# Packed attention and an ELU feed-forward: ones multiplied in TensorE's early idle time, a fourth weight buffer, stores due late, and an order chosen anew

## The chip, the core and the metric

The kernel runs on one core of a Trainium2 chip. A core has five engines that run side by side, each with its own queue of instructions worked off in order: TensorE (PE, matmuls; loading a stationary operand is a row of its own, PEld), VectorE (DVE), ScalarE (ACT), GpSimd (POOL) and SyncE (SP, which here only issues DMAs). They wait for each other through semaphores. Matmul results go to PSUM, eight banks of 128 x 512 float32; everything else lives in SBUF, 128 partitions wide. DMAs are issued on SP's queue, or on ACT's or POOL's, and run on the core's 16 DMA engines.

The metric is the device time of one launch in microseconds. The kernel before takes 708.01 us, the median of three runs (707.46 to 708.13).

## The reference

```python
def sm_attn(qq, kk, vv):
    s = scale * np.matmul(qq, kk.transpose(0, 1, 3, 2))
    s = s - np.max(s, axis=-1, keepdims=True)
    a = np.exp(s)
    a = a / (np.sum(a, axis=-1, keepdims=True) + 1e-09)
    return np.matmul(a, vv)
p_packed = sm_attn(p, k, v)             # p: 8 batches, 8 heads, 32 packed queries, 64 wide
out = sm_attn(q, p_packed, p_packed)    # q, k, v: 8 batches, 8 heads, 576 tokens, 64 wide
...
h = x @ w_in                            # x: 4608 x 512, w_in: 512 x 2048
g = np.where(h > 0.0, h, np.exp(np.minimum(h, 0.0)) - 1.0)
return g @ w_out                        # w_out: 2048 x 512
```

x is the attention's output with the heads side by side, 576 rows for each of 8 batches. All is float32.

## The kernel before, in words

**Attention.** For each batch, two softmaxes. The first (s1, line 526, or in halves, line 567) lets the 32 packed queries look at 576 keys: scores, maximum (DVE), exponential (ACT, line 550), ten transposes (line 637), the product with the values (pv, line 663), a division, one more transpose (line 689). The result, `ppT`, is at once keys and values of the second softmax. Its scores (s2, line 708) are folded so that DVE can take maximum, difference, sum and product over 32 columns (lines 716 to 758), with the exponential on ACT (line 732) between. The kernel never forms x: it multiplies `ppT` with w_in (mstep, line 809) to get M, 256 rows a batch, so that h is the second softmax `a` times M.

**Feed-forward.** Hidden units come in 16 blocks f of 128. For a visit (batch, half of its tokens, first and last block), PE computes h of one block (line 1306 in plain float32, or line 1313 as three products of parts `hi` and `lo` in the fast float32 form), ACT takes relu and exp (lines 1320, 1326), DVE puts the ELU together (line 1329), ACT and DVE split it into `hi` and `lo` (`g`), and PE adds the product with w_out's block to two PSUM banks (lines 1409 to 1412), evacuated and stored at a visit's end. A later visit to the same rows adds to what lies in HBM, with an accumulating DMA on POOL's queue (line 1455). `VISITS` is the order of batches 0 and 1, which run while the weights still come in; from batch 2 on, pairs of blocks go through a scheme of Strassen's kind (lines 1044 to 1200) with seven products in place of eight, on weights combined on the chip and kept in HBM (`sw_dram`). `S_PLAINS` names pairs computed without it. Each batch leaves 64 tokens over per half; the leftovers are kept in HBM (`rest_dram`) and multiplied with the last batch.

**Weights.** w_in and w_out arrive as 64-bit numbers, one block of 512 KB a load, into a ring of three buffers `raw` (line 347). ACT or DVE take the upper bytes (lines 342 and 320, `up` and `top`), DVE puts the float32 words together (line 367); w_out's words are split into `hi` and `lo` (`wo_a` or `wo_b`, lines 320 and 381), and only then the buffer is free.

**The order of the work.** A planner in the kernel (`schedule`) fixes the order of every engine's instructions when the kernel is built. Each piece of work is an `op` with a priority (its place in the order of blocks, moved by constants such as `T_ATT`, `LOOK`, `T_SE`), planned durations on the engines that can do it, the ops it needs and the buffers it takes. Time runs in the plan; whenever an engine is free, the ready op with the lowest priority gets it. An op's end is its start, its duration, a fixed lag of its engine (`LAG`) and a lag of its own. A DMA counts as work of one engine, `DMA`. `FIRST` lists the loads that open the plan. In the plan before, PE's durations are multiplied by `COLD` (1.9) until 3 us of dense products have run. The plan is only an order: on the chip each engine waits for what its next instruction needs, however long that takes. K, v and q of a batch share a ring of two buffers (`kvq`): q's loads wait for the values' product. All loads and plain stores are issued on SP, in the plan's order.

Of the kernel before, what the change touches and what calls it, by code (L numbers as in the profile page):

```python
# [12 lines left out]
BF16 = mybir.dt.bfloat16  # L13
# [3 lines left out]
U8 = mybir.dt.uint8  # L17
# [6 lines left out]
def packed_attention_elu_ffn(  # L24
# [22 lines left out]
    nc = tc.nc  # L47
# [15 lines left out]
    ODD_HALF = (1, 0)  # L63
    HB, SW, MIX, TOP = 2, 8, 0, 2
    FC = 512
    NFC = DFF // FC
# [11 lines left out]
    VISITS = [  # L78
# [4 lines left out]
    ]  # L83
    T_ATT = [11.5, 5.0, 17.5, 8.0, 10.0, 14.0]
    T_ATT1 = [-17.0, -14.5, -14.0, -6.0, -18.5, -13.0]
    LI = 4.0
    LO = 2.0
    LM = 1.0
    LOOK = 4.25
    TM = [26.5, 32.5, 37.5, 36.5]  # L90
    FIRST = "q v i3 k i0 i1 i2 o2".split()
    COLD = 1.9
    T_S2 = -8.0
    STAY = 19
    SWITCH = 0.105
    F_PLAIN = 0
    H_PLAIN = [0, 1]
    T_WS = 11
    T_AS = 6
    S_PLAIN = []  # L100
    S_PLAINS = {
        (2, 0): [7], (2, 1): [0], (3, 0): [1], (3, 1): [0], (4, 0): [0, 4], (4, 1): [1],
        (5, 0): [0], (5, 1): [0], (6, 0): [4], (6, 1): [7],
    }
    T_SW7 = 36
    T_ATTS = {3: [-2.5, -1.5, -5.5, 8.5, 12.0, 21.0], 4: [-1.5, 7.5, 13.5, 3.5, 10.0, 23.0], 5: [-6.5, 4, -10.5, -3.5, 12.5, 28.0], 6: [5, 10, 14.0, 3.5, 11.5, 24.5], 7: [1.0, -10, -5, 3.5, 11.5, 23.0]}
    TMS = {3: [19, 30.0, 34.5, 30.0], 4: [22, 19.5, 26.0, 27.0], 5: [11.5, 28.5, 29.0, 29.0], 6: [23, 18.5, 28.0, 23.0], 7: [16.5, 35, 30.0, 31.5]}
    T_RL = 21.0
    T_RX = 2.0
    T_HS = 20.5  # L110
    S_FIRST = (2, 0)
    T_SW = 7.5
    T_SL = 6.5
    T_SE = 15.0
    LOOK_S = 5.5
# [54 lines left out]

    def op(prio, on, fn, deps=(), take=(), use=(), after=(), mode=None, lag=0):
        o = Op()
        o.lag = lag
        o.prio, o.on, o.fn, o.deps = prio, on, fn, [d for d in deps if d is not None]
        o.after = [d for d in after if d is not None]
        o.take, o.end, o.n, o.mode = list(take), None, len(ops), mode
        for b in list(take) + list(use):
            b.users.append(o)
        ops.append(o)
        return o  # L180

    def schedule():
# [25 lines left out]
        while todo:  # L208
            for n, o in enumerate(todo[:400]):
# [12 lines left out]
                if e == "PE":  # L222
                    if dense < 3.0:
                        cost *= COLD
                        o.on = {e: cost}
                        dense += cost * (o.mode is None and cost > 1.0)
                    cost += SWITCH * (o.mode != mode)
                    mode = o.mode
                idle_at[e] = now + cost + GAP[e]
                o.start, o.end = now, now + cost + LAG[e] + o.lag  # L230
                for x, needs in o.next:
                    x.wait -= 1
                    if needs:
                        x.ready = max(x.ready, o.end)
                for r in {id(b.ring): b.ring for b in o.take}.values():
# [5 lines left out]
            else:  # L241
                ends = [o.end for o, _ in out[-400:] if o.end > now]
                ends += [t for t in idle_at.values() if t > now]
# [45 lines left out]
    for x in top_ts:  # L289
# [40 lines left out]
    def weights(f, first, prio):  # L330


        raw = ring_tile("raw", stg, [P, 8 * WC + 8], U8, "raw", bufs=3)
        up_b = ring_tile("up", stg, [P, WC], U16, "up")
# [51 lines left out]
        t = FIRST.index(name) - 60 if name in FIRST else prio - 8  # L386
        ld = op(t, {"DMA": 1.45}, load, take=[raw])
        x = op(prio, {"ACT": 0.63, "DVE": 0.42}, lift, [ld], take=[up_b], use=[raw])
# [28 lines left out]
    def attention(b, ts):  # L417
# [54 lines left out]
        def load_k(e, n):  # L472
            if n == 0:
                nc.sync.dma_start(out=p_b.t, in_=pT[b])
            if b == 0:
                nc.sync.dma_start(out=k_b[0].t, in_=kT[b])
            else:
                nc.sync.dma_start(
                    out=k_b[n].t[:, :2 * S].rearrange("p (c s) -> p c s", c=2),
                    in_=kT[b, :, 2 * n:2 * n + 2, :],  # L480
                )

        def load_v(e, n):
            x = v_b[n].t
            nc.sync.dma_start(
                out=x[:, :2 * E].rearrange("p (c e) -> p c e", c=2),
                in_=v[b, 2 * n * P:2 * (n + 1) * P, :].rearrange("(c p) e -> p c e", p=P),
            )
            nc.sync.dma_start(
                out=x[:S - 4 * P, 2 * E:], in_=v[b, 4 * P:, n * E // 2:(n + 1) * E // 2]  # L490
            )

# [431 lines left out]
    def strassen_weights(u):  # L924
# [35 lines left out]
        for n, b in enumerate(sw):  # L960
# [13 lines left out]
            y = op(prio, {"DVE": 0.41}, low, [y], use=[t_b, b])  # L974
            s_ready[u, n] = op(prio, {"DMA": 0.7}, store, [y], use=[b])

# [14 lines left out]
    def keep_leftover(b, f, o, prio):  # L991
        run["hb"] = o
        hb_done[b].append(o)
        if f % 2:
            x = hb[b]

            def store(e):
                nc.sync.dma_start(out=rest_dram[b // 4, f // 2, :, :, b % 4 // 2, b % 2, :], in_=x.t)

            rest_done[b, f // 2] = op(prio - T_HS, {"DMA": 0.5}, store, hb_done[b], use=[x])  # L1000

# [11 lines left out]
    def strassen_pair(i, b, win, f):  # L1013
# [210 lines left out]
        if last:  # L1224
# [37 lines left out]
            y = op(q, {"DVE": 0.42}, add3, [y], use=[part, acc[1]])  # L1262
            y = op(q, {"DVE": 0.69}, add4, [y, acc[2].last], use=[part, acc[2]])
            y = op(q, {"DVE": 0.42 if both or rest else 0.69}, add5, [y, acc[3].last], use=[part, acc[3]])
# [5 lines left out]

            def store(e):
                for r in range(2):
                    nc.sync.dma_start(
                        out=out[t0 + r * step:t0 + r * step + P, :], in_=part.t[:, r * E:(r + 1) * E]
                    )

            op(q, {"DMA": 1.4}, store, [y], use=[part])

    acc = None
    for i, (b, win, f) in enumerate(order):  # L1280
# [140 lines left out]
        if final:  # L1421
# [25 lines left out]
            for a, (r0, r1) in zip(acc, rows):  # L1447
# [59 lines left out]
```

## Time and profile before

| | |
|---|---|
| median of three runs | 708.01 us (707.46 to 708.13) |
| the profiled execution's own time | 708.88 us |
| its span, first to last instruction | 706.3 us |
| mean granted clock of TensorE | 0.987 |
| DMA | 167.79 MB, 238 GB/s over the span |

The span is 2.6 us shorter than the execution that it belongs to; what lies around it is start and end of the launch. A busy PE in the profile is not always a PE at its peak: the ends of matmuls are modelled, and a matmul of the same shape takes about twice as long while the granted clock is 0.5.

Three groups of the page show the size of the instructions that fill most of the span: `L1200 PE MATMUL psum<-sw,g` with 1212 instructions and 183.7 us, `L1135 DVE TENSOR_TENSOR g<-w,g` with 96 and 99.6 us, `L320 ACT CAST g<-w` with 96 and 86.6 us. The DMA part of the page has 340 loads of combined weights of 256 KB each (3.9 us from issue to landing), 32 loads of weights of 512 KB (4.6 and 4.8 us), and 22 accumulating stores on POOL's queue (5.4 us).

### The profile page before, as it was taken

Reading aid. Unit: us, or ns where it says so; the run is one execution under the profiler, and the core shown is the slowest. Engines: PE = TensorE matmul, PEld = TensorE weight load, DVE = VectorE, ACT = ScalarE, POOL = GpSimd, SP = SyncE. Lnnn points to the kernel's source line nnn. Section 1 sums busy time; section 2 is a strip of 40 time slices with the busy share of each in tenths; the row PEclk is TensorE's granted clock in tenths of the full one; section 3 lists DMA queues with packets and bytes.
Section 4 is the critical chain, followed back from the end, with each engine's and each line's share of the span. In section 5 each row is a group of like instructions: output and inputs, shape, how many; then the busy total and the mean of one; then the engine's idle time right before and its main releaser. Section 6 shows DMA issues by size and latency. Waiting matters only on the chain.

```text
span 706.3 us, 16075 instructions
## 1 busy us (share of the span) xinstructions
PE 675.5 (96%) x6051; PEld 593.9 (84%) x6051; DVE 576.3 (82%) x1284; ACT 454.8 (64%) x888; POOL 21.1 (3%) x30
## 2 busy tenths in 40 slices
PE   3599998998999999999999999999999999999996
PEld 2376886785879988998989988898899988999996
DVE  1898665998988998778987879779986999878874
ACT  4899998785667557755674557665665566555441
POOL 0000011102010000000000000000000000000000
PEclk9889999999999999999999999999999999999999
DMA  8877777579399956969788777798788787675863
GB/s 324 279 238 248 237 196 153 122 203 290 125 268 295 314 182 199 318 194 312 245 262 267 242 212 231 240 274 270 250 285 299 224 274 235 194 219 158 293 206 124
DMA packets 102797, 167.79 MB, mean 238 GB/s; under 512 B 26176, under 2 KB 35392, under 8 KB 102464
## 3 DMA queue, kind: packets, MB, share of 16 engines
q1 hardware_dynamic: 99552, 160.99, 70.5%
q0 software_dynamic: 3168, 5.77, 5.3%
q8 instruction: 48, 0.79, 0.4%
q14 instruction: 29, 0.24, 0.1%
HBM read 138.94 MB, written 27.79 MB: 236 GB/s over the span
## 4 chain that ended last, share of the span: by engine, by line
PE 83%; ACT 6%; DMA 5%; DVE 3%; issue 1%; SPq 1%; DVEq 0%; ACTq 0%
PE psum L1200 40%; PE psum L1044 22%; PE psum L809 4%; PE psum L1313 4%; PE psum L1409 3%; PE psum L1410 2%; PE psum L1412 2%; DMA raw<-in_w_out 2%; PE psum L663 2%; DMA raw<-in_w_in 1%; PE psum L1306 1%; DMA kvq<-in_qT 1%; PE psum L708 1%; PE psum L637 1%; PE psum L567 1%
## 5 line engine op out<-in xcount | busy, mean ns | idle before, releaser
L1200 PE MATMUL psum<-sw,g 128*128 128x256 f32 x1212 | 183.7, 283 | 0.0
L1200 PEld LDWEIGHTS psum<-sw,g 128*128 128x128 f32 x1212 | 160.7, 189 | 9.5 <-issue 7.0
L1135 DVE TENSOR_TENSOR g<-w,g 128x896 fp32r<-128x896 f32 (+1 forms) x96 | 99.6, 1039 | 28.4 <-ACT g L320 28.0
L320 ACT CAST g<-w 128x896 fp32r<-128x896 f32 (+1 forms) x96 | 86.6, 903 | 52.9 <-PE psum L1200 23.4
L1044 PE MATMUL psum<-a_hi,m_hi 128*128 128x256 f32 (+1 forms) x384 | 115.5, 301 | 0.0
L1044 PE MATMUL psum<-a_hi,m_lo 128*128 128x256 f32 (+1 forms) x384 | 113.5, 296 | 0.0
L1044 PE MATMUL psum<-a_lo,m_hi 128*128 128x256 f32 (+1 forms) x384 | 113.4, 295 | 0.0
L1200 PE MATMUL psum<-wo_a,g 128*128 128x256 f32 (+1 forms) x537 | 90.7, 299 | 0.4 <-ACT e L1059 0.4
L1126 DVE TENSOR_TENSOR w<-w 128x128 f32<-128x128 f32 (+1 forms) x255 | 84.8, 333 | 6.4
L1200 PE MATMUL psum<-wo_b,g 128*128 128x256 f32 (+1 forms) x534 | 84.8, 288 | 0.0
L1200 PEld LDWEIGHTS psum<-wo_a,g 128*128 128x128 f32 x537 | 75.9, 189 | 5.8 <-issue 1.8
L1044 PEld LDWEIGHTS psum<-a_hi,m_hi 128*128 128x128 f32 x384 | 72.7, 189 | 8.7 <-issue 2.7
L1056 ACT ACTIVATE e<-psum 128x320 f32<-128x320 f32 x96 | 41.7, 436 | 57.4 <-PE psum L1044 54.9
L1200 PEld LDWEIGHTS psum<-wo_b,g 128*128 128x128 f32 x534 | 73.1, 189 | 4.5 <-issue 3.4
L1044 PEld LDWEIGHTS psum<-a_lo,m_hi 128*128 128x128 f32 x384 | 72.6, 189 | 0.2
L1044 PEld LDWEIGHTS psum<-a_hi,m_lo 128*128 128x128 f32 x384 | 72.6, 189 | 0.0
L1056 ACT ACTIVATE w<-psum 128x512 f32<-128x512 f32 x48 | 28.6, 598 | 41.4 <-PE psum L1044 23.4
L1051 DVE SCALAR_TENSOR_TENSOR w<-e,psum 128x256 f32<-128x256 f32 x96 | 39.8, 415 | 15.8 <-ACT e L1059 15.5
L1059 ACT ACTIVATE e<-e 128x320 f32<-128x320 f32 x96 | 45.1, 472 | 2.6
L822 DVE TENSOR_TENSOR m_lo<-psum,m_hi 128x1024 fp32r<-128x1024 f32 (+1 forms) x36 | 37.1, 1038 | 7.1 <-ACT m_hi L320 7.1
L1051 DVE SCALAR_TENSOR_TENSOR w<-w,psum 128x512 f32<-128x512 f32 x48 | 32.5, 678 | 10.5 <-ACT w L1059 10.3
L320 ACT CAST m_hi<-psum 128x1024 fp32r<-128x1024 f32 (+1 forms) x36 | 31.1, 875 | 12.0 <-PE psum L809 11.3
(121 smaller groups left out, 1156.7 us busy)
## 6 DMA issues: line engine op xcount, KB each, us to landing
sw<-sw_dram SPq DMA_DIRECT2D x340, 256.0 KB, 3.9
raw<-in_w_in SPq DMA_DIRECT2D x16, 512.0 KB, 4.6
kvq<-in_v SPq DMA_DIRECT2D x16, 512.0 KB, 5.7
raw<-in_w_out SPq DMA_DIRECT2D x16, 512.0 KB, 4.8
out<-part SPq DMA_DIRECT2D x32, 256.0 KB, 3.4
sw_dram<-sw SPq DMA_DIRECT2D x32, 256.0 KB, 5.5
kvq<-in_kT SPq DMA_DIRECT2D x14, 576.0 KB, 5.0
kvq<-in_qT SPq DMA_DIRECT2D x14, 576.0 KB, 5.5
```

Of the source, the lines that this page charges most:

```text
L320: (nc.scalar.copy if e == "ACT" else nc.vector.tensor_copy)(out=out, in_=in_)
L809: nc.tensor.matmul(ps.t[cols_of(pair), g, :w], lhsT=st.ppT.t[rows_of(g), pair, :], rhs=w_in_sb[rows_of(g), pair, c * FC + part * w:c * FC ...
L822: nc.vector.tensor_tensor(out=m_b[1].t[:, :, fs], in0=ps.t[:, :, :w], in1=m_b[0].t[:, :, fs].bitcast(F32), op=ALU.subtract,)
L1044: nc.tensor.matmul(ps, lhsT=m_b[p].t[:, g, o:o + P], rhs=st.a.t[q][:, g, cols], start=(n == 0), stop=(n == 3 * G - 1),)
L1051: nc.vector.scalar_tensor_tensor(out=out, in0=e_, scalar=-1.0, in1=ps, op0=ALU.add, op1=ALU.max)
L1056: nc.scalar.activation(out=out, in_=ps, func=AF.Relu, scale=-1.0)
L1059: nc.scalar.activation(out=x, in_=x, func=AF.Exp, scale=-1.0)
L1126: nc.vector.tensor_tensor(out=out, in0=x, in1=y, op=o)
L1135: nc.vector.tensor_tensor(out=g_b.all[:, 7 * P:(7 + b1 - b0) * P], in0=blocks(b0, b1), in1=g_b.all[:, :(b1 - b0) * P].bitcast(F32), op=ALU ...
L1200: nc.tensor.matmul(a.t[:, at * H:at * H + rhs.shape[-1]], lhsT=operand(blk, p), rhs=rhs, start=new and n == k == 0, stop=a.final == (u, mi ...
L1313: nc.tensor.matmul(ps_b.t[:, :n_tok], lhsT=m_b[x].t[:, g, o:o + P], rhs=st.a.t[y][:, g, cols], start=(n == 0), stop=(n == 3 * G - 1),)
L1409: nc.tensor.matmul(a.t, lhsT=g_b.t[0][:, t], rhs=wo(f, 0), start=first, stop=False)
```

## The change

Ten edits.

1. **Ones.** The tile `part_sb` is filled with ones by DVE at the start. Read as bfloat16, its first 256 columns are both operands of a matmul into a PSUM bank that nothing reads (`fill`). From 1.5 us of planned time on, whenever nothing else is planned for PE, the planner puts in one such matmul, of a planned 0.11 us, until dense products (h or w_out's, over 0.6 us each) of 3 us in all have been planned. Then the bank is given back. `COLD` is gone: real work is planned at its full-clock durations.
2. **Late stores.** Ops can be `late`: whoever needs such an op, or the buffers that it uses, counts on its end; dependents add 1.5 us. Stores get it, except the last batch's.
3. **Accumulating stores** count as 1.7 us of DMA with 2.8 us of lag, in place of 1.0 us of POOL. They are still issued on POOL's queue.
4. **Four buffers** for arriving weights, in place of three, with 0.4 us of lag for a load.
5. **v in one transfer.** The host lays v out so that each half is one load with 5 KB in each partition (64 KB of it padding), in place of two loads.
6. **p of batch 0** is issued on ACT's queue.
7. **The store of a Strassen visit** is two ops of one DMA each: rows 128 to 255 after the fourth addition, rows 0 to 127 after the fifth. Before, both were issued after the fifth.
8. **Leftovers' stores** count as 0.3 us in place of 0.5.
9. **One more pair plain** at visit (2, 0), and another pair plain at (6, 0).
10. **Order and due times** chosen anew: three neighbouring pairs of visits swap, and nearly all constants of the priorities differ.

```diff
-        (0, 0, 0, 4), (0, 1, 0, 4), (1, 0, 0, 4), (1, 1, 0, 4),
+        (0, 0, 0, 4), (0, 1, 0, 4), (1, 1, 0, 4), (1, 0, 0, 4),
         (1, 1, 4, 8), (1, 0, 4, 8), (0, 1, 4, 8), (0, 1, 8, 12),
-        (0, 0, 4, 8), (0, 0, 8, 12), (1, 0, 8, 12), (0, 1, 12, 16),
-        (1, 1, 8, 16), (1, 0, 12, 16), (0, 0, 12, 16),
+        (0, 0, 4, 8), (0, 0, 8, 12), (0, 1, 12, 16), (1, 0, 8, 12),
+        (1, 1, 8, 16), (0, 0, 12, 16), (1, 0, 12, 16),
...
-    FIRST = "q v i3 k i0 i1 i2 o2".split()
-    COLD = 1.9
+    FIRST = "i2 k q v i1 i3 i0".split()
+    T_FILL = 1.5
...
-    T_RL = 21.0
-    T_RX = 2.0
-    T_HS = 20.5
+    T_RL = -3.0
+    T_RX = 0.5
+    T_HS = 41.5
...
+    def fill(e):
+        x = part_sb[:, 0, :E // 4].bitcast(BF16)
+        nc.tensor.matmul(fill_b.t[:, :E // 2], lhsT=x[:, :P], rhs=x, start=True, stop=True)
...
                     if dense < 3.0:
-                        cost *= COLD
-                        o.on = {e: cost}
-                        dense += cost * (o.mode is None and cost > 1.0)
+                        dense += cost * (o.mode is None and cost > 0.6)
+                        fill_end.end = now if dense >= 3.0 else None
...
-                        x.ready = max(x.ready, o.end)
+                        x.ready = max(x.ready, o.end + x.late)
...
+                if fill_end.end is None and now >= T_FILL and idle_at["PE"] <= now:
+                    o = Op()
+                    o.on, o.fn, o.deps, o.mode, o.lag = {"PE": 0.11}, fill, [], None, 0
...
+                    out.append((o, "PE"))
+                    continue
...
+    nc.vector.memset(part_sb[:, 0, :], 1.0)
...
-        raw=3, up=2, top=TOP, p=2, ppT=2, pp=1, k0=1, q0=1,
+        raw=4, up=2, top=TOP, p=2, ppT=2, pp=1, k0=1, q0=1,
...
-                nc.sync.dma_start(out=p_b.t, in_=pT[b])
+                (nc.sync if b else nc.scalar).dma_start(out=p_b.t, in_=pT[b])
...
-            x = v_b[n].t
...
+            nc.sync.dma_start(out=v_b[n].t, in_=v[b, n])
...
+            for r, z in ((1, y4), (0, y)):
+                op(q, {"DMA": 0.7}, lambda e, r=r: store(e, r), [z], use=[part], late=LATE * (b < B - 1))
...
-                eng = {"POOL": 1.0} if visits[v_n][2] > 0 else {"DMA": 0.7}
-                stores[r0] = op(i + LOOK, eng, store, [y, stores.get(r0)], use=[part])
+                again = visits[v_n][2] > 0
+                stores[r0] = op(
+                    i + LOOK, {"DMA": 1.7 if again else 0.7}, store, [y, stores.get(r0)], use=[part],
+                    lag=2.8 * again, late=LATE,
+                )
```

More of the change, by code (lines that the diff above doesn't have):

```diff
@@ L64, in packed_attention_elu_ffn @@
     HB, SW, MIX, TOP = 2, 8, 0, 2
+    LATE = 1.5
     FC = 512
@@ L78, in packed_attention_elu_ffn @@
     VISITS = [
[1 row of a table removed]
[1 row of a table added]
         (1, 1, 4, 8), (1, 0, 4, 8), (0, 1, 4, 8), (0, 1, 8, 12),
[2 rows of a table removed]
-    ]
[L84 to L90, printed above, removed]
-    FIRST = "q v i3 k i0 i1 i2 o2".split()
-    COLD = 1.9
-    T_S2 = -8.0
-    STAY = 19
[2 rows of a table added]
+    ]
+    T_ATT = [5.5, 0.5, 17.0, 10.0, -5.5, 16.0]
+    T_ATT1 = [-22.0, -10.5, -21.5, -13.5, -21.5, -9.0]
+    LI = 3.5
+    LO = 1.5
+    LM = 1.5
+    LOOK = 4.0
+    TM = [25.5, 32.5, 37.0, 33.5]
+    FIRST = "i2 k q v i1 i3 i0".split()
+    T_FILL = 1.5
+    T_S2 = -21.0
+    STAY = 15
     SWITCH = 0.105
@@ L169, in packed_attention_elu_ffn, with op @@
     LAG = {"PE": 0.27, "DVE": 0.05, "ACT": 0.05, "DMA": 2.2, "POOL": 5.0, "CTL": 0.0}
-    def op(prio, on, fn, deps=(), take=(), use=(), after=(), mode=None, lag=0):
+    def op(prio, on, fn, deps=(), take=(), use=(), after=(), mode=None, lag=0, late=0):
         o = Op()
-        o.lag = lag
+        o.lag, o.late = lag, late
         o.prio, o.on, o.fn, o.deps = prio, on, fn, [d for d in deps if d is not None]
@@ L241, in schedule @@
             else:
-                ends = [o.end for o, _ in out[-400:] if o.end > now]
+                if fill_end.end is None and now >= T_FILL and idle_at["PE"] <= now:
+                    o = Op()
+                    o.on, o.fn, o.deps, o.mode, o.lag = {"PE": 0.11}, fill, [], None, 0
+                    o.late, o.prio, o.n = 0, 0, 0
+                    o.take = [] if fill_b.users[1:] else [fill_b]
+                    if o.take:
+                        if not R["psum"].grant(o.take, now):
+                            raise ValueError
+                        R["psum"].take(o.take, now)
+                    fill_b.users.append(o)
+                    o.start, o.end = now, now + 0.11
+                    idle_at["PE"] = o.end
+                    out.append((o, "PE"))
+                    continue
+                ends = [o.end + t for o, _ in out[-700:] for t in (0, LATE) if o.end + t > now]
                 ends += [t for t in idle_at.values() if t > now]
@@ L330, in weights @@
     def weights(f, first, prio):
-        raw = ring_tile("raw", stg, [P, 8 * WC + 8], U8, "raw", bufs=3)
+        raw = ring_tile("raw", stg, [P, 8 * WC + 8], U8, "raw", bufs=4)
         up_b = ring_tile("up", stg, [P, WC], U16, "up")
@@ L386, in weights @@
         t = FIRST.index(name) - 60 if name in FIRST else prio - 8
-        ld = op(t, {"DMA": 1.45}, load, take=[raw])
+        ld = op(t, {"DMA": 1.45}, load, take=[raw], lag=0.4)
         x = op(prio, {"ACT": 0.63, "DVE": 0.42}, lift, [ld], take=[up_b], use=[raw])
@@ L974, in strassen_weights @@
             y = op(prio, {"DVE": 0.41}, low, [y], use=[t_b, b])
-            s_ready[u, n] = op(prio, {"DMA": 0.7}, store, [y], use=[b])
+            s_ready[u, n] = op(prio, {"DMA": 0.7}, store, [y], use=[b], late=LATE)
     for u in range(NF // 2):
@@ L998, in store @@
                 nc.sync.dma_start(out=rest_dram[b // 4, f // 2, :, :, b % 4 // 2, b % 2, :], in_=x.t)
-            rest_done[b, f // 2] = op(prio - T_HS, {"DMA": 0.5}, store, hb_done[b], use=[x])
+            rest_done[b, f // 2] = op(
+                prio - T_HS, {"DMA": 0.3}, store, hb_done[b], use=[x], late=LATE
+            )
     def g_buf():
@@ L1262, in strassen_pair @@
             y = op(q, {"DVE": 0.42}, add3, [y], use=[part, acc[1]])
-            y = op(q, {"DVE": 0.69}, add4, [y, acc[2].last], use=[part, acc[2]])
+            y = y4 = op(q, {"DVE": 0.69}, add4, [y, acc[2].last], use=[part, acc[2]])
             y = op(q, {"DVE": 0.42 if both or rest else 0.69}, add5, [y, acc[3].last], use=[part, acc[3]])
@@ L1269, in strassen_pair, with store @@
                 run["rest5"].deps.append(acc[3].last)
[L1271 to L1277, printed above, removed]
+            def store(e, r):
+                nc.sync.dma_start(
+                    out=out[t0 + r * step:t0 + r * step + P, :], in_=part.t[:, r * E:(r + 1) * E]
+                )
+            for r, z in ((1, y4), (0, y)):
+                op(q, {"DMA": 0.7}, lambda e, r=r: store(e, r), [z], use=[part], late=LATE * (b < B - 1))
     acc = None
@@ L1484, in pairs_T, with values @@
         )
+    def values(x):
+        out = np.zeros((B, 2, 128, 2 * E + E // 2), x.dtype)
+        for n in range(2):
+            for c in range(2):
+                out[:, n, :, c * E:(c + 1) * E] = x[:, (2 * n + c) * 128:(2 * n + c + 1) * 128]
+            out[:, n, :S - 512, 2 * E:] = x[:, 512:, n * E // 2:(n + 1) * E // 2]
+        return out
     arrays = {
@@ L1488 @@
         "in_kT": pairs_T(k),
-        "in_v": np.ascontiguousarray(v.transpose(0, 2, 1, 3).reshape(B, S, H * D)),
+        "in_v": values(v.transpose(0, 2, 1, 3).reshape(B, S, H * D)),
         "in_pT": pairs_T(p),
```

31 lines of the change are left out of this document (14 added, 17 removed).

## The prediction

> **What bounds the kernel now.** I read the page first, then the stretches by stage, the granted clock at single places, the chain of waits, and the timeline of the head and the tail. The page:
>
> ```profile
> span 706.3 us, 16075 instructions
> PE 675.5 (96%) x6051; PEld 593.9 (84%) x6051; DVE 576.3 (82%) x1284; ACT 454.8 (64%) x888; POOL 21.1 (3%) x30
> ```
>
> TensorE (PE) is the bound: 96% of the span. A change like this can only win where PE stands idle or runs slowly, so I cut the span into stretches; the columns are length, then busy time of each engine, granted clock, DMA share.
>
> ```profile
> core 0: us, PE busy (x) PEld busy (x) DVE busy (x) ACT busy (x) POOL busy (x), PEclk, DMA share, GB/s
> 0.00:35.00 35.00, 16.91 (x265) 10.19 (x269) 18.44 (x38) 22.14 (x46) 1.62 (x8) 0.93 0.85 300
> 35.00:40.00 5.00, 5.00 (x72) 4.00 (x64) 4.28 (x11) 4.46 (x12) 0.00 (x0) 0.50 0.71 243
> 40.00:110.00 70.00, 68.12 (x454) 52.25 (x454) 55.25 (x127) 67.12 (x155) 3.67 (x4) 1.00 0.73 221
> 110.00:120.00 10.00, 7.44 (x39) 6.21 (x38) 4.68 (x13) 7.01 (x17) 0.82 (x2) 0.93 0.66 191
> 120.00:170.00 50.00, 50.00 (x461) 40.67 (x468) 48.13 (x121) 38.46 (x98) 8.04 (x10) 0.98 0.76 183
> 170.00:180.00 10.00, 7.73 (x77) 4.36 (x62) 7.05 (x16) 5.49 (x11) 1.76 (x2) 0.83 1.03 318
> 180.00:700.00 520.00, 519.63 (x4706) 475.78 (x4705) 436.19 (x961) 310.09 (x554) 5.23 (x6) 1.00 0.76 241
> 700.00:706.30 6.30, 0.68 (x6) 0.47 (x5) 2.24 (x5) 0.00 (x0) 0.00 (x0) 0.95 0.43 166
> ```
>
> The 520 us from 180 on have 0.4 us of idle PE: nothing to win. What is lost lies in four places: the head (18.1 us idle of 35, then 5 us at half clock), 110 to 120 (2.6 idle), 170 to 180 (2.3 idle), the tail (5.6 idle). From 40 to 110 ACT is nearly as full as PE (67.1 and 68.1 of 70), so there a faster PE alone wins little. The granted clock around these gaps:
>
> ```profile
> 19.00:23.00 4.00, 3.53 (x64) 1.78 (x64) 3.09 (x6) 2.65 (x6) 0.00 (x0) 0.58 0.98 350
> ...
> 40.00:42.00 2.00, 2.00 (x16) 1.33 (x23) 1.85 (x4) 2.00 (x6) 0.00 (x0) 0.97 1.11 401
> ...
> 119.00:122.00 3.00, 3.00 (x10) 2.71 (x11) 1.94 (x5) 3.00 (x8) 1.75 (x2) 0.50 0.58 53
> 122.00:123.00 1.00, 1.00 (x6) 0.75 (x4) 0.61 (x2) 0.86 (x3) 0.00 (x0) 0.98 1.05 191
> ```
>
> The chain of waits (start, us) says when PE took up work before those stretches, and how long two matmul groups take at full clock:
>
> ```profile
> 34.50 2.31 PE psum L663 x72
> ...
> 118.94 1.65 PE psum L1313 x6
> ...
> 147.93 1.13 PE psum L526 x32
> ...
> 163.65 1.39 PE psum L663 x80
> ```
>
> After an idle gap the clock is 0.5 and comes back only after continuous work: PE restarts at 118.9 and is at 0.98 in 122 to 123, some 3.4 us later; it restarts at 34.5, is at 0.50 all through 35 to 40 and at 0.97 in 40 to 42, some 5.6 us later. Timeline of PE in the head:
>
> ```profile
> 7.92 2.17 PE L526 MATMUL psum<-k,p 64*32 64x288 f32 x32 [7.92 <-DMA k<-in_kT]
> 12.20 2.37 PE L637 MATMUL psum<-ident,tmp 128*128 128x128 f32 x10 [2.10 <-ACT tmp L550]
> 14.49 2.42 PE L663 MATMUL psum<-kvq,tmp 128*32 128x64 f32 x80
> ...
> 27.15 1.97 PE L1306 MATMUL psum<-k,m_hi 128*128 128x256 f32 x8 [0.47 <-DVE k L758]
> 30.72 1.49 PE L637 MATMUL psum<-ident,tmp 128*128 128x128 f32 x10 [1.61 <-ACT tmp L550]
> ```
>
> So the head runs cold: 2.17 against 1.13 for the first scores, 2.42 against 1.39 for the values, and for ten transposes 2.37 against 1.49 at 30.7. (The clock column has 0.93 over the first 35 us; the durations say that it does not see all of this.)
>
> **The change, part by part.**
>
> **1. Ones in the head.** What they can save on the chain from k's landing to the first dense product at 27.15: scores 1.04, transposes 0.88 (half of it on the chain, since the first group of five is evacuated while the second runs: 0.45), values 1.03, and half a microsecond of the second scores at 19 to 21 us (clock 0.58 there). Together about 3.0. After that, 35 to 40 at clock 0.50 loses 2.5 us of full-clock work, and 34.5 to 35 another 0.25: 2.75 in all. ACT is 4.46 of 5 busy and DVE 4.28 there, so not all of it passes: I take 2.0.
>
> What they cost. A one is planned at 0.11 us. No row has it; nearest is the dense stream:
>
> ```profile
> 683.35 15.57 PE psum L1200 x132
> ```
>
> 0.118 us for 256 columns at full clock, about 0.236 at half. The ones are a fixed number, issued in order ahead of real work, so PE must get through all of them. They are planned from 1.5 us of the planner's time, which I set 0.7 behind the span's (estimate), so from 2.2; up to k's landing at 7.92 fit 52. At full clock they take 6.1 us; the cold stretch adds half of 3.4 to 5.6 us, 1.7 to 2.8. They need only one 128x512 memset on an idle DVE and start somewhere between 1 and 2.2 (I take 1.6), so they end at 9.4 to 10.5: the first scores start 1.5 to 2.6 late, I take 2.1. Some 90 more lie between there and the fourth dense product (estimate: about 16 us idle in all by then, over 0.11, less 52); at 0.008 over plan each, 0.7. So 3.0 + 2.0 - 2.8: a **gain of 2.2**. Bounds: a loss of 1 (nothing passes ACT and DVE, wake-up at its slowest) and a gain of 5 (the whole 2.75, wake-up in 3.4 us, ones at plan).
>
> The Trainium skill ("TensorE: Matmul & The Clock Gate", Part 1: The HAM clock gate) says that the clock needs one full busy window of about 3.4 us, and that the windows run freely. By it the wake-up would take 3.4 to 6.8 us and the ones would end up to 0.6 us later than by my rows; the sum would fall by 0.3. The 3.4 and 5.6 us above agree.
>
> **2. Four weight buffers.**
>
> ```profile
> 108.40 6.49 DMA raw<-in_w_out
> ```
>
> ```profile
> 114.91 0.65 ACT L342 ACTIVATE up<-raw 128x512 uint16<-128x512 uint8 x1 [2.99 <-DMA raw<-in_w_out]
> ```
>
> ```profile
> L347 SPq DMA_DIRECT2D raw<-in_w_out x11: 328/337/592, 49.4 to 112.1; - x11
> L347 SPq DMA_DIRECT2D raw<-in_w_in x10: 323/336/541, 41.9 to 99.7; - x10
> ```
>
> The load at 108.4 waited for its buffer, took 6.5 us, and ACT stood 2.99 us; PE then idled 2.5 and ran 3.4 us at half clock. Price 2.6 + 1.7 = 4.3. The 21 loads from 41.9 to 112.1 come one per 3.5 us, so a fourth buffer gives 3.5 us of lead, more than 2.99. What is late next is ACT's own work (67.1 of 70 us busy before it), so I take **3.0** (0 to 4.3). In the head the fourth buffer lets the last of the first four loads be issued without waiting for a conversion; the DMA is at its rate there (share 0.85 over 35 us, 300 GB/s), and q's transfer covers it, so I count nothing; without that cover it would be one load, 1.7 us (512 KB at 300 GB/s).
>
> **3. Stores due late, accumulating stores counted as transfers, new order.** These add no instruction, but move loads.
>
> ```profile
> 165.76 7.47 DMA kvq<-in_qT
> ```
>
> q of a batch waits until the values' matmuls free its buffer, then takes 7.5 us among stores; in 170 to 180 PE idles 2.27, and the clock of 0.83 loses 1.7: 4.0. The new accounting tells the planner of that traffic, but the ring of two buffers remains and stays the cause. I take **1.5** (-2 to 4). Three neighbouring pairs of visits swap, and batch 1's loads, queued on SP among weight loads and stores, move with their due times. The leftovers' call is due 24 places later than before (behind its use, no longer ahead); it can still go early, since the DMA has room (share 0.76 from 180 on, 0.43 at the end); uncovered it would stop PE by at most a load like the 6.5 us one above, less its lead.
>
> One more pair is computed plain: 12 matmuls in place of 21.
>
> ```profile
> 391.01 2.79 PE psum L1200 x12
> ```
>
> 21 at 0.118 are 2.48 us: **+0.3**, on PE's path.
>
> **4. v in one transfer, p on ACT's queue, two halves of a store.** v's two issues become one: 16 fewer on SP, off the path; each carries 64 KB of padding, 16 x 64 KB = 1 MB, 3.5 us of transfer at 300 GB/s over the run, hidden where the DMA share is 0.76. p's issue goes to an ACT that idles 12.9 of the first 35 us; nothing. The tail:
>
> ```profile
> 701.26 1.01 DVE L1231 TENSOR_TENSOR part<-part,psum 128x512 f32<-128x512 f32 x2
> 701.37 0.81 SPq L1273 DMA_DIRECT2D out<-kvq  x2
> 702.30 0.89 SPq L1273 DMA_DIRECT2D out<-part  x2
> ```
>
> Both last issues wait for the last addition; afterwards only one does: **0.45** saved (0 to 0.45).
>
> **Sum.** -2.2 - 3.0 - 1.5 + 0.3 - 0.45 = -6.9. The profiled execution took 708.9 (span 706.3); 702.0 there. The median of 708.0 lies 0.9 below the profiled run, so **701.1**; own range 696 to 706, from the bounds taken not all at once.
>
> **Rivals.**
>
> *ACT and DVE hold the head.* PE's new speed is swallowed by them: 67.1 of 70 us on ACT from 40 to 110 speaks for it, 12.9 us of idle ACT before 35 against. The head gives 0, q's stall stays: 708.0 - 3.0 - 0.45 + 0.3 = **704.9**.
>
> *The change doesn't do what it says.* The ones stop at 3 us of dense products, PE idles again and is cold; the new order has its own late load where the old ones were, since SP issues in order and a load behind a waiting store gains nothing from a fourth buffer. Only the tail and the plain pair stay: **707.9**. For it: the clock was 0.50 in 35 to 40 although dense products had run at 27.15. Against it: 2.99 us of ACT's wait has a plain cause.
>
> *Slower: the ones are a queue in front of real work.* If PE stays at half clock under them, each takes about 0.236. The other parts bring 4.65, so it is slower than before from a lateness of 4.65 plus the noise, 6 us, at the fourth product: over 140 ones that is 0.11 + 0.045, a mean above 0.155. At 0.17 it is 8.4 late with nothing won: 708.0 - 4.65 + 8.4 = **711.8**. For it: PE was cold at 14.5 after 4.5 us of work with a gap in it. Against: at 118.9 it woke in 3.4 us of plain matmuls.
>
> **How the numbers follow.** Forecast 0.62, ACT and DVE 0.17, doesn't do it 0.09, slower 0.10, a larger gain than the own range (both stalls and the whole head) 0.02. A measurement of this kernel can tell about 0.2%, 1.4 us: faster is below 706.6. Faster takes the forecast, the larger gain, most of the second (0.14) and a little of the third (0.03): 0.81; same 0.09; slower 0.10. The range leaves out half the slow case and the far end of gains: 695 to 710.
>
> **What would show it.** Right: first scores last near 1.13, clock 1.00 through 20 to 42, the first dense product ahead of 27 us, no ACT wait of 3 us on a weight near 110, one issue behind the last addition. Wrong: first scores later than 10.6 (ones too slow); clock 0.5 in 30 to 40; PE idle as long as before in 100 to 180; PE idle beyond 180, where the order had none.

## The result and the profile after

The changed kernel takes **700.18 us** (median of four, 699.53 to 701.61) against 708.07 us for the kernel before (median of four, 707.46 to 709.32): a ratio of 0.9889, 95% interval 0.9869 to 0.9909, 7.9 us less. The profiled execution took 700.24 us. Its page begins:

```profile
span 698.2 us, 16294 instructions
PE 686.1 (98%) x6197; PEld 604.8 (87%) x6197; DVE 573.6 (82%) x1282; ACT 455.3 (65%) x888; POOL 21.1 (3%) x30
```

PE is busier than before although the kernel is shorter: the ones count as work. So the stretches matter, not the sum. The view by windows of the kernel after (length, then busy time of each engine, granted clock, DMA share):

```profile
core 0: us, PE busy (x) PEld busy (x) DVE busy (x) ACT busy (x) POOL busy (x), PEclk, DMA share, GB/s
0.00:35.00 35.00, 32.77 (x482) 24.99 (x483) 20.21 (x44) 23.52 (x49) 1.62 (x8) 1.00 0.86 325
35.00:40.00 5.00, 3.21 (x19) 2.41 (x17) 4.12 (x9) 5.00 (x13) 0.00 (x0) 1.00 0.84 273
40.00:110.00 70.00, 68.53 (x479) 51.90 (x480) 55.17 (x127) 68.02 (x155) 3.67 (x4) 1.00 0.78 232
110.00:120.00 10.00, 9.48 (x53) 8.00 (x52) 7.47 (x18) 9.82 (x24) 1.75 (x2) 1.00 0.52 96
120.00:170.00 50.00, 49.95 (x461) 40.26 (x461) 49.51 (x129) 35.49 (x92) 8.67 (x10) 1.00 0.84 224
170.00:180.00 10.00, 10.00 (x59) 8.74 (x58) 9.93 (x25) 6.48 (x18) 0.00 (x0) 1.00 0.68 186
180.00:690.00 510.00, 509.66 (x4633) 466.20 (x4632) 423.42 (x930) 306.57 (x543) 5.36 (x6) 1.00 0.76 243
```

Two of the four losing places are gone. In 110 to 120 PE idles 0.5 us in place of 2.6, and the 3.4 us at half clock behind that gap (1.7 us of work) are gone too: 3.7 us. In 170 to 180 it idles not at all in place of 2.3 us, at clock 1.00 in place of 0.83: 4.0 us. The span shrank by 8.1, so with the 0.3 us of the plain pair about 0.7 us is left for everything else, the head included.

The head, PE's timeline of the kernel after:

```profile
1.46 5.22 PE L185 MATMUL psum<-part 128*128 128x256 bf16 x27 [1.46 <-DVE ebias L297]
7.45 1.20 PE L539 MATMUL psum<-k,p 64*32 64x288 f32 x32 [0.77 <-DMA k<-in_kT]
8.59 2.47 PE L185 MATMUL psum<-part 128*128 128x256 bf16 x21
...
13.71 1.46 PE L676 MATMUL psum<-kvq,tmp 128*32 128x64 f32 x80
...
25.16 1.03 PE L1321 MATMUL psum<-k,m_hi 128*128 128x256 f32 x4
...
37.18 1.02 PE L1321 MATMUL psum<-k,m_hi 128*128 128x256 f32 x4
40.39 0.72 PE L721 MATMUL psum<-kvq,ppT 64*32 64x288 f32 x16 [2.19 <-DMA kvq<-in_qT]
```

and the same two last pieces of work in PE's timeline of the kernel before:

```profile
40.81 1.03 PE L1306 MATMUL psum<-k,m_hi 128*128 128x256 f32 x4
41.76 0.72 PE L708 MATMUL psum<-kvq,ppT 64*32 64x288 f32 x16
```

The scores last 1.20 us in place of 2.17, the values 1.46 in place of 2.42, and the first dense product starts at 25.16 in place of 27.15. The lead grows to 3.6 us (40.81 less 37.18). Then PE stands 2.19 us for q of batch 1, a wait that before did not have, and the lead is 1.4 us. The chain of waits of the kernel after runs through that transfer:

```profile
33.48 6.78 DMA kvq<-in_qT
```

The stall at 170 to 180 went another way. SP's queue in the kernel before, then in the kernel after:

```profile
165.07 2.07 SPq L497 DMA_DIRECT2D kvq<-in_qT  x2
```

```profile
156.88 1.39 SPq L510 DMA_DIRECT2D kvq<-in_qT  x2
```

PE's timeline before, where the second half of the scores waits for that q, and after, from the values' product that frees the buffer to the scores:

```profile
173.37 1.21 PE L708 MATMUL psum<-kvq,ppT 64*32 64x288 f32 x16 [2.27 <-DMA kvq<-in_qT]
```

```profile
155.40 1.46 PE L676 MATMUL psum<-kvq,tmp 128*32 128x64 f32 x80
...
164.37 1.20 PE L721 MATMUL psum<-kvq,ppT 64*32 64x288 f32 x32
```

The new order has the values' product at 155.4, 8.2 us earlier than before (163.65 in the prediction's chain). So q is issued 8.2 us earlier, other products fill the 7.5 us from its issue to the scores, and all 32 score matmuls follow without an idle gap on PE.

The tail: the chain of waits ends, before and after, in the same addition on DVE:

```profile
701.94 0.33 DVE part L1231
```

```profile
693.80 0.33 DVE part L1246
```

```profile
694.29 0.41 SPq L1287 DMA_DIRECT2D out<-part  x1
```

Only one issue stands behind it now, as the third fence shows (SP's queue after, a view cut to 694.3 to 694.9; the other of the pair was issued at 693.86). Yet from that addition to the end of the span it is 4.4 us in both kernels (706.3 less 701.94, 698.2 less 693.80).

### The profile page after: what moved, and what is told of

It is laid out like the page before. It is cut to its first block, busy times and chain, and to the rows that moved or that the text cites. A ratio compares the mean times of both kernels' runs of the same rounds, so it can differ in the third digit from the quotient of the medians.

```text
span 698.2 us, 16294 instructions
## 1 busy us (share of the span) xinstructions
PE 686.1 (98%) x6197; PEld 604.8 (87%) x6197; DVE 573.6 (82%) x1282; ACT 455.3 (65%) x888; POOL 21.1 (3%) x30
## 4 chain that ended last, share of the span: by engine, by line
PE 91%; ACT 4%; DVE 2%; DMA 2%; issue 1%; DVEq 0%; SPq 0%; ACTq 0%
PE psum L1215 41%; PE psum L1059 22%; PE psum L822 5%; PE psum L1328 4%; PE psum L1424 3%; PE psum L1425 3%; PE psum L1427 3%; PE psum L185 2%; PE psum L676 2%; PE psum L1321 2%; PE psum L721 1%; PE psum L650 1%; DMA kvq<-in_qT 1%; PE psum L580 1%; DMA k<-in_kT 1%
## 5 line engine op out<-in xcount | busy, mean ns | idle before, releaser
L1215 PE MATMUL psum<-sw,g 128*128 128x256 f32 x1200 | 179.0, 282 | 0.0
L1215 PEld LDWEIGHTS psum<-sw,g 128*128 128x128 f32 x1200 | 157.6, 189 | 7.3 <-issue 4.7
L1215 PE MATMUL psum<-wo_a,g 128*128 128x256 f32 (+1 forms) x543 | 93.8, 304 | 0.0
L1215 PEld LDWEIGHTS psum<-wo_a,g 128*128 128x128 f32 x543 | 77.9, 189 | 7.0 <-issue 2.6
L1215 PEld LDWEIGHTS psum<-wo_b,g 128*128 128x128 f32 x519 | 71.5, 189 | 4.9 <-issue 3.9
L822 PE MATMUL psum<-w_in_sb,ppT 64*32 64x512 f32 (+1 forms) x640 | 35.8, 513 | 0.0
```

The lines of the kernel that those rows point to most:

```text
L822: nc.tensor.matmul(ps.t[cols_of(pair), g, :w], lhsT=st.ppT.t[rows_of(g), pair, :], rhs=w_in_sb[rows_of(g), pair, c * FC + part * w:c * FC ...
L1215: nc.tensor.matmul(a.t[:, at * H:at * H + rhs.shape[-1]], lhsT=operand(blk, p), rhs=rhs, start=new and n == k == 0, stop=a.final == (u, mi ...
```

## The experiments

Each kernel was timed beside the kernel before on the same chip; ratios are to that, with 95% intervals. 0.001 is 0.7 us. "In the order of" a kernel means that each engine's instructions are exactly that kernel's but for the edit.

**Without the ones, in the order of after.**

```diff
-        nc.tensor.matmul(fill_b.t[:, :E // 2], lhsT=x[:, :P], rhs=x, start=True, stop=True)
+        return
```

> The kernel after, with the same order of every other instruction, but the 167 ones are not issued. Theory A (the prediction's step 1: ones save about 5 us of cold time and cost about 2.8, net 2.2): the time rises by about 2, to 702.4, the first scores take 2.2 us again and the clock shows 0.5 in places before 40 us. Theory B (the order behind the head was chosen for a warm head, so the whole cold time of 5 to 6 us comes back): 705 to 706. Theory C (the head is held by transfers, ACT and DVE, and the ones buy nothing): 699.5 to 700.9, no change that can be told.

702.11 us, ratio 0.9933 (0.991 to 0.9957), 0.0044 or 3.1 us slower than with them (0.9 to 5.3 by the two intervals). Its windows and PE's waits show part of it:

```profile
160.00:170.00 10.00, 8.63 (x97) 5.54 (x96) 9.50 (x21) 5.51 (x13) 1.76 (x2) 1.00 0.95 285
```

```profile
PE psum L822 <- DVE w_in_sb L387: 3.6, 1, 3.6
PE psum L721 <- DMA kvq<-in_qT: 2.9, 3, 1.6
```

The wait for q at 165 us comes back: 1.4 us of the 10 are idle, where after has 0.05 in 50. In the head, the scores of batch 1 start at 40.52, hardly later than the 40.39 of after: there the late q had eaten the difference already. So the ones are worth some 3 us in this order, and in these profiles half of it is seen some 130 us behind them. Why there stays open: from 41 to 160 us PE is only 0.1 us later at the same matmul than in after, and q was issued 0.1 us later, but its two halves took 8.0 and 8.9 us to land, in after 5.3 and 7.1.

**Each one twice, in the order of after.**

```diff
         nc.tensor.matmul(fill_b.t[:, :E // 2], lhsT=x[:, :P], rhs=x, start=True, stop=True)
+        nc.tensor.matmul(fill_b.t[:, :E // 2], lhsT=x[:, :P], rhs=x, start=True, stop=True)
```

> The kernel after with every one issued twice, the order otherwise the same: some 170 ones of 0.11 us more, 18.7 us of added work for TensorE in the head. If the ones are a queue in front of real work (the slower rival of the prediction), nearly all of the added time after the first scores shows: the 27 added ones ahead of the scores find 0.8 us of slack plus a warmer clock, the other 140 have none, so plus 13 to 16 us, 713 to 716. If ACT, DVE and transfers hold the head and TensorE has slack between its pieces, less than 8 us shows: below 708.

717.31 us, ratio 1.0153 (1.0126 to 1.0181): 0.0264 or 18.7 us above after, more than the 13 to 16 expected. The 167 added ones would be 18.7 us at the 0.112 us that one takes at full clock (33 in 3.71 us in the chain of after). So about all of what they take ends up in the time: ones do queue in front of real work, and a plan that gives them too short a duration pays for it. At 0.112 against a planned 0.11 it doesn't.

**Every second one left out, in the order of after.**

```diff
+    nth = itertools.count()
+
     def fill(e):
+        if next(nth) % 2:
+            return
```

> The kernel after with every second one left out, all else in place. If the ones cost time where they stand in front of real work (prediction: 0.7 us for being longer than planned), this is up to 1 us faster than after, as long as the clock stays at 1.00. If the clock falls because TensorE is then idle half of the time between its pieces, it goes the way of the kernel without ones, 2 to 3 us slower than after (ratio to before 0.992 to 0.993).

699.52 us, ratio 0.9897 (0.9874 to 0.9921): the same as after. PE's timeline:

```profile
1.46 3.17 PE L189 MATMUL psum<-part 128*128 128x256 bf16 x14 [1.46 <-DVE ebias L301]
7.43 2.17 PE L543 MATMUL psum<-k,p 64*32 64x288 f32 x32 [2.80 <-DMA k<-in_kT]
```

The first scores run cold here (2.17, in after 1.20), and only from 10.3 us on are ones as short as at full clock. Even so, batch 1's second scores start at 37.96, in after at 40.39: fewer ones stand in front of them. At 163.8 PE waits 1.0 us for the same q as without the ones, which takes half of its lead over after. So the time needs neither warm first scores nor every gap filled.

**Ones in the plan of before.** The planner of before, with the ones added to it as in the change, and all else left (`COLD` too).

```diff
+                if fill_end.end is None and now >= 1.5 and idle_at["PE"] <= now:
+                    o = Op()
+                    o.on, o.fn, o.deps, o.mode, o.lag = {"PE": 0.11}, fill, [], None, 0
...
+                    out.append((o, "PE"))
+                    continue
...
+    nc.vector.memset(part_sb[:, 0, :], 1.0)
```

> The kernel before with ones in the idle time of its own order (its planned durations stay the cold ones, so every other instruction keeps its place), until 3 us of dense products are planned. Theory A: about 2 us faster than before, 706, clock 1.00 up to the last one. Theory B (the ones carry most of the gain): 4 to 6 us faster, 702 to 704. Theory C (the head is held by others): within 1 us of before, 707 to 709.

709.82 us, ratio 1.006 (1.0029 to 1.0091). The expectation's premise did not hold: the planner, which now gives a bank to the ones and has more points in planned time, made another order (some 800 of PE's 6051 real matmuls are not those that stand at the same place in before), so this run says nothing of the ones alone. PE's timeline of its profile shows one thing all the same:

```profile
1.46 5.75 PE L184 MATMUL psum<-part 128*128 128x256 bf16 x30 [1.46 <-DVE ebias L299]
10.00 2.18 PE L548 MATMUL psum<-k,p 64*32 64x288 f32 x32 [2.79 <-DMA k<-in_kT]
```

With 2.8 us of idle time behind 30 ones the scores ran as slowly as with no ones (2.17).

**Ones alone, in the order of before.** 122 ones put into the idle gaps of before's plan, into banks that stand free there.

```diff
-        for o, e in schedule():
+        for o, e in with_ones(schedule()):
```

> The kernel before in exactly its order on every engine; only 122 ones are put between TensorE's instructions, where its plan has idle time from 4.05 us on up to the fourth dense product. This is edit 1 alone. Prediction's step 1: 2 us faster than before (ratio 0.997), bounds 5 faster to 1 slower. If the ones only pay in an order chosen for a warm head: within 1 us, or slower by 1 to 3 as the ones stand in front of work that comes sooner than its cold plan says.

707.39 us, ratio 1.0007 (0.9993 to 1.0021): nothing. PE's timeline, then ACT's, then PE's waits:

```profile
7.60 1.21 PE L527 MATMUL psum<-k,p 64*32 64x288 f32 x32 [0.85 <-DMA k<-in_kT]
...
13.55 1.46 PE L664 MATMUL psum<-kvq,tmp 128*32 128x64 f32 x80
...
20.55 2.17 PE L709 MATMUL psum<-q,ppT 64*32 64x288 f32 x32
```


```profile
14.90 0.67 ACT L343 ACTIVATE up<-raw 128x512 uint16<-128x512 uint8 x1 [1.81 <-DMA raw<-in_w_in]
...
17.58 0.65 ACT L343 ACTIVATE up<-raw 128x512 uint16<-128x512 uint8 x1 [1.17 <-DMA raw<-in_w_in]
18.14 0.29 ACT L676 ACTIVATE pp<-psum,ri 128x64 f32<-128x64 f32 x1
```

```profile
PE psum L690 <- ACT pp L676: 3.0, 1, 3.0
```

The scores last 1.21 us and the values start at 13.55 in place of 14.49. But in before's order two conversions of weights stand on ACT ahead of the division. They wait for weights, so the division ends no earlier than with a cold PE (18.14, before 17.30), and the second scores start at 20.55, before at 19.18. Six ones (1.15 us) stand in front of them too, and after the 3.0 us of idle time they run at half clock (0.50 from 19.9 to 23.0). The head's gain is lost at an engine that works in order behind a transfer.

**Four buffers alone, in the order of before.**

```diff
-        raw = ring_tile("raw", stg, [P, 8 * WC + 8], U8, "raw", bufs=3)
+        raw = ring_tile("raw", stg, [P, 8 * WC + 8], U8, "raw", bufs=4)
```

> The kernel before in exactly its order, but four real buffers for arriving weights, so each load on SP's queue waits for one release earlier. This is edit 4 alone. Prediction's step 2: 3 us faster (ratio 0.996), ACT's wait of 3 us near 112 to 115 and TensorE's idle time at 116 to 119 are gone. Rival: the load stands behind other waiting instructions on SP's queue in the old order, so it is issued no earlier and the time stays within 1 us; the wait then went away through the new order.

703.04 us, ratio 0.9945 (0.9922 to 0.9968): 3.9 us faster. Its windows:

```profile
110.00:120.00 10.00, 9.54 (x53) 7.98 (x52) 5.79 (x16) 8.71 (x22) 1.75 (x2) 1.00 0.79 183
120.00:170.00 50.00, 47.15 (x468) 36.81 (x474) 49.22 (x124) 37.47 (x94) 8.88 (x10) 1.00 0.79 199
170.00:180.00 10.00, 10.00 (x72) 7.65 (x57) 7.08 (x15) 5.01 (x11) 0.00 (x0) 0.83 0.89 285
```

The stall at 110 to 120 is gone: at the same matmuls PE's lead over before grows there from 1.3 us (at 113.7) to 4.9 (at 118.1), so by 3.6. Elsewhere this profile wins and loses: 2.0 ahead at the head's end, 1.2 of it lost near 100. In the second scores near 170 PE still stands: 2.85 us idle in 120 to 170, and the clock of 0.83 behind it. 2.40 of that is put down to DVE here, but q's second half lands only 0.2 us before PE goes on.

**Ones and four buffers, in the order of before.** Both edits above.

> Both edits above together in the order of before. Sum of the prediction's steps 1 and 2: 5 us faster (ratio 0.993). If the order is what matters: within 1.5 us of before, with the stall of TensorE at 170 to 173 in place.

703.16 us, ratio 0.9939 (0.9918 to 0.996). The ones add nothing that can be measured to the buffer, and the 2.9 us for which PE waits for the division stay.

**Three buffers, in the order of after.** The planner still counts four.

```diff
-        raw = ring_tile("raw", stg, [P, 8 * WC + 8], U8, "raw", bufs=4)
+        raw = ring_tile("raw", stg, [P, 8 * WC + 8], U8, "raw", bufs=3)
```

> The kernel after in exactly its order, but with three real buffers for arriving weights in place of four; the planner still counts four, so loads stand on SP's queue where they stood and wait there for the third buffer back. Prediction's step 2 (the fourth buffer takes away ACT's wait of 3 us and the idle and cold time behind it): plus 3 us or more, 703 to 705, with TensorE idle again between 90 and 120. Rival (the new order alone took the wait away): within 1 us of 700.2.

726.36 us, ratio 1.0275 (1.024 to 1.031): 0.0386 or 27 us above after. SP's queue and the windows:

```profile
32.59 10.04 SPq L367 DMA_DIRECT2D raw<-in_w_in  x2
42.73 1.34 SPq L510 DMA_DIRECT2D kvq<-in_qT  x2
```

```profile
40.00:110.00 70.00, 60.12 (x367) 44.42 (x366) 47.98 (x106) 57.36 (x130) 0.00 (x0) 0.93 0.59 190
```

The second of two weight loads waits 10 us on SP for its buffer, and q of batch 1 stands behind it: issued at 42.73, in after at 33.48. From 40 to 110 PE is idle 9.9 us, in after 1.5. At the same matmuls PE is 7 us behind after near 41 us, 15 near 81 and 25 near 142. So the price of a buffer was 3.9 us in the old order and 27 in the new: an order made for four loads in flight leans on the fourth.

**The division first, in the order of before.** A theory for the ones' missing gain: it hangs on the place of batch 0's division on ACT. Here the two divisions, the transpose, its copy and the first half of the second scores stand right behind the values' product, ahead of the two conversions; no ones.

```diff
+        want, got = ["norm", "norm", "tr2", "tr2c", "s2"], []
+        for o, e in plan[at + 1:]:
+            if want and o.fn.__name__ == want[0]:
+                got.append((o, e))
+                want.pop(0)
...
-        for o, e in schedule():
+        for o, e in pp_first(schedule()):
```

> The kernel before, without ones, its order changed in one place: for batch 0 the division of the values, its transpose, the copy to ppT and the first half of the second scores stand right behind the values' matmuls on ACT, so ahead of the conversion of two arriving weights that stood in front of them. New theory (ones alone gained nothing, since ACT stood 1.8 and 1.2 us for arriving weights with the division queued behind): without ones the values end at 16.9, when those weights have landed, so little is gained, 0 to 1 us (ratio 0.9985 to 1.0). Rival (ACT's order alone was the fault, cold or warm): 2 us or more faster (ratio below 0.997).

709.25 us, ratio 1.0029 (1.0012 to 1.0046): slower, which neither the theory nor its rival had said. By its profile, M waits 2.3 us for a weight.

**The same with the ones.**

> The same change of order together with the 122 ones. New theory: now the warm head's time passes on: the division starts near 15.1 in place of 18.1, the second scores near 17 in place of 20.5, and the whole is 2 to 3 us faster than before (ratio 0.996 to 0.997). Rival (ACT's and DVE's work in the head is the bound in any order): within 1 us of before, as with the ones alone.

708.88 us, ratio 1.003 (1.0011 to 1.0048): the theory fell. PE's timeline shows why:

```profile
16.89 1.39 PE L709 MATMUL psum<-q,ppT 64*32 64x288 f32 x32
20.15 0.67 PE L810 MATMUL psum<-w_in_sb,ppT 64*32 64x256 f32 x16 [1.87 <-DVE w_in_sb L368]
...
26.46 1.19 PE L527 MATMUL psum<-kvq,p 64*32 64x288 f32 x8 [3.13 <-DMA kvq<-in_kT]
...
31.68 2.08 PE L1307 MATMUL psum<-k,m_hi 128*128 128x256 f32 x8
```

The second scores do come at 16.9 (20.55 above). Then M waits for weights, since their conversions now come later; k of batch 1 is late by 3.1 us, and the first dense product is at 31.68, later than before. My reading is that the three buffers come free later with the conversions, and so the loads behind them on SP; with four buffers, in the next run, PE's waits have no entry for that k.

**The same with ones and four buffers.**

> Ones, that place in ACT's order, and four weight buffers, all else in the order of before. If the gains add: 3.9 for the buffer and 2 to 3 for the ones, ratio 0.990 to 0.992, near the kernel after (0.989), and the rest of the new order would be worth 1 us or less. If the remaining stalls are matters of the new order alone: 0.993 to 0.995, as without that change of place.

703.72 us, ratio 0.9956 (0.9935 to 0.9977), no better than four buffers alone. Its head, by windows:

```profile
20.00:42.00 22.00, 16.89 (x233) 12.23 (x241) 20.37 (x41) 19.81 (x43) 0.00 (x0) 1.00 0.76 257
```

The mean granted clock of this run is 0.999, as high as in after, and it is worth nothing: PE still idles 5.1 us between 20 and 42, now warm.

**The old accounts, with the constants of after.** Stores no longer late, accumulating stores counted on POOL again, the leftovers' stores at 0.5; the planner then makes another order.

```diff
-    LATE = 1.5
+    LATE = 0.0
...
-                    i + LOOK, {"DMA": 1.7 if again else 0.7}, store, [y, stores.get(r0)], use=[part],
-                    lag=2.8 * again, late=LATE,
+                    i + LOOK, {"POOL": 1.0} if again else {"DMA": 0.7}, store, [y, stores.get(r0)], use=[part],
+                    lag=0, late=LATE,
```

> The kernel after with its constants, but stores not due late, accumulating stores counted as 1.0 of POOL again and leftovers' stores as 0.5; the order is planned again with that, so it differs in places. Prediction's step 3 (the accounts help to keep transfers apart, 1.5 us with the order): 1 to 2 us slower than after, ratio 0.991 to 0.992. If the accounts matter more than that, waits for q or for a weight come back, 0.994 or more. If not at all: 0.989.

706.48 us, ratio 0.9988 (0.997 to 1.0005), with ones and four buffers in place. PE's waits:

```profile
PE psum L721 <- DMA kvq<-in_qT: 3.4, 2, 2.3
PE psum L1424 <- DVE hb L1344: 2.0, 1, 2.0
```

The late q is back: the 2.3 us are at 168.6. The 2.0 us of the second line, at 104.5, go back to a late weight: ACT waited 1.84 us for a load of w_in that took 6.39, and DVE's ELU, which PE's product needs, came behind it. (In the kernel a `late` op is itself ready only 1.5 us after what it needs: it is the store that is planned later, and not what depends on the store, as is said further up.) The gain hangs on an order that was fitted to its accounts; the constants were chosen together with them, so this run doesn't part the two.

## Why the prediction was right, and where it was not

The forecast was 701.1 us; it is 700.18. The sign, the place of two stalls and the sum (6.9 forecast, 7.9 measured) held. The split did not, and that the sum came so close is in part luck: 2.2 for the ones and 1.5 for the order were reckoned as gains of their own, and only the pair brings 4.0. With four buffers in all of them, four kernels part the ones from the order (the new order has the small edits to v, p and the stores with it):

| four buffers | without ones | with ones |
|---|---|---|
| order of before | 0.9945 | 0.9939 |
| order of after | 0.9933 | 0.9889 |

The buffer alone is 3.9 us of the 7.9. The ones alone and the new order alone add under 1 us each, within the intervals; together they add 4.0 (0.9945 less 0.9889, times 707). That 4.0 is clear of the intervals. That the two are worth more together than one by one is not: the difference is 0.0038, and the four intervals leave some 0.004 either way.

1. **The ones, forecast 2.2.** The speeds were right: the 3.0 us of chain and the cold stretch at 34.5 to 40 were found and removed, and the lead at 37 us was 3.6. The first mis-sized term is "the first scores start 1.5 to 2.6 late, I take 2.1": they start at 7.45, when k lands, after PE has waited 0.77 us for it, so they are not late at all. I filled the time to k's landing with 52 ones; the trace has 27, because the planner's time had no event between 1.5 and 4.05 us at which to put one, while on the chip they start at 1.46. So 27 ones planned for 3 us could take 5.2. That error would have made the gain larger by 2.1. The step that failed is the next one: that what PE saves is kept but for a part ("not all of it passes: I take 2.0"). I weighed only ACT's and DVE's busy shares against it. In before's order it is lost at a division that stands behind two late weights, and with the division moved ahead at the weights and k behind it; in the new order 2.2 of 3.6 us are lost to q of batch 1, whose transfer then ends last. All of these are transfers that no faster PE moves. The 2.2 lies inside what the ones measured in the new order (0.9 to 5.3 us), but not by this way: there PE's lead over the kernel without them is 0.1 us at 41 us. What remains in the span for the head is about 0.7 us in my account of the windows. "PE's new speed is swallowed" was a rival with ACT and DVE as the holders; the swallowing came, by other holders.
2. **Four buffers, forecast 3.0 (0 to 4.3).** Measured 3.9 alone, interval 2.3 to 5.5. Place, mechanism and price hold (3.6 us at the place): in the kernel after, ACT's timeline near 110 has its conversions without a wait,

```profile
108.61 0.71 ACT L362 ACTIVATE up<-raw 128x512 uint16<-128x512 uint8 x1
...
110.44 0.71 ACT L362 ACTIVATE up<-raw 128x512 uint16<-128x512 uint8 x1
```

   and it was nearer the full price than my cut to 3.0 for "ACT's own work". Of the lead of 3.5 us per load 3.3 came: in before's order the load issued at 108.4 is issued at 105.1 with the fourth buffer. That an order could come to lean on it for 27 us I did not see.
3. **Stores, accounts, order, forecast 1.5 (-2 to 4).** It is the upper end: the 4.0 us at 165.8 to 173.4 are gone whole. The sentence that failed is "the ring of two buffers remains and stays the cause". The ring remains, but the order can empty it sooner: the values' product moved up 8.2 us and dense products cover the transfer. But it only just lands in time: without the ones, and with half of them, the same order waits for q again, by 1.4 and 1.0 us. The table suggests that this gain and that of the ones are one gain, and that to give each a line of its own in the sum was the wrong form; that is not shown. How much of it is due to the accounts and how much to the constants stays open; the new order with the old constants was not run.
4. **v, p, the tail, forecast 0.45.** As foreseen, one issue is left behind the last addition, and inside the span it brings nothing: 4.4 us from that addition to the end in both. v's one transfer, p's queue and the plain pair were not run by themselves.

The rivals: that the change does nothing falls with the 3.7 and 4.0 us. That the ones are a queue in front of real work is half true. Each one does push what is behind it, as the doubled ones show, but the mean one took 0.125 us (27 in 5.22 us, the other 140 at 0.112), under the 0.155 from which it would have decided. Of the signs I had named, all those for the forecast came (scores of 1.20, clock 1.00 in 20 to 42, dense products at 25.2, no wait of ACT near 110, one issue in the tail); none of those against it did, and PE idles 0.3 us in the 510 from 180 on.

None of the kernels that were run is faster than after by more than the intervals tell; with half the ones it is as fast.

## What to carry to other kernels

Before adding up what single edits save, ask what each is worth in the order it will run in: here warm multiplies and a new order added under 1 us singly, within the intervals, and 4 us together, and a buffer was worth 4 us in one order and 27 in another. To measure one edit of a planned kernel, hold the order fixed and splice the edit in; a planner that is run again answers another question. When an engine is made faster in a pipeline's start, look for the in-order queue (of an engine or of DMA issues) where a transfer stands ahead of the work that was gained.

## What the runs showed of the hardware that was not expected

**The clock column starts late.** A window of the kernel after, and the group of all ones:

```profile
1.40:4.00 2.60, 2.54 (x13) 1.79 (x14) 0.01 (x2) 1.26 (x2) 0.76 (x3) 1.00 0.85 237
```

```profile
L185 PE MATMUL psum<-part 128*128 128x256 bf16 x167 | 22.6, 291 | 1.5 <-DVE ebias L297 1.5
```

The column says 1.00 from the start, but one by one in the trace the ones' starts lie 0.213 us apart up to 5.70 us and 0.110 from 5.86 on. So PE starts cold unseen: 20 of the 27 were cold, and full clock came 4.3 us after the first one. This differs from run to run: with every one doubled the spacing falls to 0.11 at 4.1 us, 2.6 after the first. The group's mean of 291 ns is a modelled length of a pipelined matmul; spacing, not that mean, is a one's price.

The Trainium skill ("TensorE: Matmul & The Clock Gate", Part 1: The HAM clock gate) asks for one busy window of about 3.4 us, of windows that run freely; my estimate from that is a wake-up of 3.4 to 6.8 us. The 4.3 agree, the 2.6 do not. The same part sets the ramp at under 1% of a typical span and advises against fitting to a count of cold matmuls. The runs agree: the ratio with ones is 1.0007 in the order of before, and in the order of after the ones are worth 0.4%.

**Half the multiplies hold a warm clock once it is there, and it can be worth nothing.** With every second one left out, the ones are 0.213 us apart up to 10.15 us and 0.11 from 10.27 on, and from there to the tail the clock stays up; the mean of 0.998 counts the cold start as warm. And of the kernels with before's order and four buffers, the one with a mean clock of 0.999 is no faster than the one with 0.993 (ratios 0.9956 and 0.9945).

**Time around the span.** It is 2.0 to 2.1 us in the median of every kernel with after's edits, 2.5 to 2.6 in before and in before with four buffers, and between, 2.2 to 2.5, where ones run in the order of before. So some 0.5 us of the gain lies outside the span. No run here parts its causes; the tail's edit is not the only candidate, since those kernels do without it.
